# Sixteen moves of one-hot codes, issued from ScalarE's queue instead of SyncE's, in a clustered attention with a feed-forward layer

## The chip, the cores and the metric

The kernel runs on one core of a Trainium2 chip. The metric is the device time of one execution in microseconds; the kernel before takes 299.18 us (median of three runs, 299.0 to 299.66). Each engine has an instruction queue of its own and works through it in order; an instruction that waits holds up whatever stands behind it on its engine. PE is TensorE, DVE VectorE, ACT ScalarE, POOL GpSimd, SP SyncE. SP does no arithmetic: in this kernel it issues most of the transfers.

## The reference, cut to what matters

Attention over 4 batches, 8 heads, 768 positions of 64 numbers, in which a query sees a key only if both belong to the same of 16 clusters; then a SiLU layer over the heads put side by side.

```python
q_assign = np.argmax(np.einsum('bhsd,hcd->bhsc', q_n, c_n), axis=-1)
k_assign = np.argmax(np.einsum('bhsd,hcd->bhsc', k_n, c_n), axis=-1)
mask = q_assign[:, :, :, None] == k_assign[:, :, None, :]
scores = np.where(mask, scale * np.matmul(q, k.transpose(0, 1, 3, 2)), -1000000000.0)
attn = softmax(scores)                       # over the keys
x = (attn @ v).transpose(0, 2, 1, 3).reshape(B * S, H * D)
h = x @ w_in;  out = (h / (1 + exp(-h))) @ w_out
```

## The kernel before

**The work on one head.** A *job* is the rows of q and k of one head: jobs 0 to 7 are batch 0, 8 to 15 batch 1, and so on; two further jobs, `x0` and `x1`, hold half of the queries of batch 0 for four heads each. The rows are loaded (`raw`), split into a high and a low 16-bit half (`hi` L97, `lo` L110, tile `hl`) and transposed into the tile `ab`, which has 128 rows: on PE with an eviction in the opening (`tr`, `ev`), by a DMA transpose from SP in batch 1 (`xpose`, L121). From `ab` PE computes the sixteen logits of each row (L159); DVE takes the maximum (`mxn`, L183) and compares (`om`, L192), which gives a one-hot code for the cluster.

**The move.** The code has to stand below the data, in rows 64 to 79 of the same tile `ab`, because the score product (`qk_mm`, L325) then adds a large negative number wherever clusters differ. For that PE transposes the code into PSUM (`cd_mm`, L221, tiles `psN` or `psC`); `cd_ev` copies it into a tile `cd` of 80 or 96 partitions, on ACT (L232) or on DVE (L234); and a DMA (L235) carries `cd` into rows 64 to 79 of `ab`, 40 or 48 KB. This is done for sixteen jobs: 2 to 7, x0 and x1 in the opening, 8 to 15 in batch 1. No `qk_mm` that reads this `ab` can start before the move has landed. (Jobs 0 and 1 write their codes in place, and batches 2 and 3 take another way, with `c_move` on POOL.)

**What follows.** ACT turns each score tile into exponentials (`exp`, L330, tile `P`); the score tile `pS` has two buffers, so `qk_mm` of unit u waits for the exponential of unit u-2. PE multiplies with v (`pv`, L342); then come the first matrix of the layer (L390), tanh on ACT (L402), a gate on DVE (L405) and the second matrix (L417, L477).

**What sets the order.** It is written out by hand: `plan` is a list of words, each of which calls one helper, so every engine's order is that of the words. `ce2.A` is `cd_ev` of job 2 with the eviction on ACT, `ce5.D` that of job 5 on DVE; `xe0`, `xe1` are those of the x jobs. `ex4` is an exponential, `qk4` its product, `ht14` the DMA transpose of job 14, `r10` the loads of job 10, `vl6` a load of v. SP issues its DMAs in the order of the plan as well: a move stands on SP's queue behind all loads, transposes and stores that the plan names before it.

**The semaphores of the DMAs.** The program gives the transfers of SP and ACT eight semaphores in turn, DMAHW0 to DMAHW7 in the rows below. A transfer does not start before the one that had its semaphore last, eight transfers earlier in the plan, has landed. This wait is taken by the queue that issues the transfer.

Of the kernel before, what the change touches and what calls it, by code (L numbers as in the profile page):

```python
# [29 lines left out]
def kernel(  # L30
# [52 lines left out]
    raws, hls, abs_ = {}, {}, {}  # L83
# [141 lines left out]
    def cd_ev(job, eng):  # L225
        m = (job.n + 1) // 2
        cd = mp.tile([6 * HC, 256], f16, name="cd", bufs=4)
        psN = psNs.pop(job.name)
        o, i = cd[0 : m * HC], psN[0 : m * HC, 256:512]
        add = 0.0 if job.name[0] == "x" else kadd[0 : m * HC, m - 5 : m - 4]  # L230
        if eng == "A":
            nc.scalar.activation(out=o, in_=i, func=AF.Identity, bias=add, scale=OHV)  # L232
        else:
            nc.vector.tensor_scalar(out=o, in0=i, scalar1=OHV, scalar2=add, op0=ALU.mult, op1=ALU.add)  # L234
        nc.sync.dma_start(abs_[job.name][64 : 64 + HC, 0 : 2 * m, :].rearrange("p n c -> p (n c)"), o)  # L235
# [368 lines left out]
    def step(op, n, eng, banks):  # L604
# [225 lines left out]
```

## Time and profile before

| what | us |
|---|---|
| median of three runs | 299.18 |
| the three runs | 299.18, 299.66, 299.0 |
| span of the profiled execution, first to last instruction | 297.9 |
| PE busy | 288.7 |
| ACT busy | 233.2 |
| DVE busy | 223.8 |
| idle time of PE before score products (L325) | 2.2 |

The page gives no time for the profiled execution besides its span; the runs lie 1.1 to 1.8 us above it. Times in the profile count from the start of the span. The opening is the first 40 us or so, batch 1's codes are made between 60 and 95 us. "SPq" and "ACTq" are the queues that issue DMAs; the duration of such a row is the issue alone, and the landing is given apart.

### The profile page before, as it was taken

What the parts mean: (1) busy time and instruction counts of PE and PEld (TensorE: products, weight loads), DVE (VectorE), ACT (ScalarE), POOL (GpSimd) and SP (SyncE); (2) the same over time, 40 slices, a digit from 0 to 9 for tenths busy, and PEclk for the clock granted to TensorE, in tenths of its full rate; (3) what the DMA queues carried; (4) which work ended last, traced back from release to release, by engine and by line L of the source; (5) the groups of instructions that cost most, each with busy time, mean ns of one, the idle gap of its engine ahead of it and who ended that gap; (6) DMA issues with size and microseconds to landing.
All of it is one profiled execution on the core that took longest, in us unless ns stands there. A gap on an engine that the chain in (4) does not pass through costs nothing.

```text
span 297.9 us, 8577 instructions
## 1 busy us (share of the span) xinstructions
PE 288.7 (97%) x3433; PEld 212.6 (71%) x3433; DVE 223.8 (75%) x489; ACT 233.2 (78%) x406; POOL 68.7 (23%) x124
## 2 busy tenths in 40 slices
PE   7899999999979999999999999999999999999995
PEld 3767766666658887777866887767867886777684
DVE  5898849689979986989467897788656733666663
ACT  5998999965979878999789876898669768964731
POOL 2655804000227001334444024220420000000000
PEclk9999999999999999999999999999999999999999
DMA  6999999999997899795399535867221102211103
GB/s 214 286 256 247 179 201 176 193 247 216 171 300 178 171 176 257 176 151 131 102 202 213 164 66 114 256 165 113 51 89 35 26 2 74 82 29 35 39 19 125
DMA packets 75208, 44.13 MB, mean 148 GB/s; under 512 B 54288, under 2 KB 70960, under 8 KB 75168
## 3 DMA queue, kind: packets, MB, share of 16 engines
q1 hardware_dynamic: 70272, 35.75, 50.3%
q0 software_dynamic: 4608, 7.54, 13.5%
q8 instruction: 27, 0.44, 0.6%
q10 hardware_dynamic: 288, 0.30, 0.3%
q14 instruction: 13, 0.11, 0.1%
HBM read 27.30 MB, written 6.29 MB: 113 GB/s over the span
## 4 chain that ended last, share of the span: by engine, by line
PE 87%; DMA 5%; ACT 3%; DVE 3%; issue 1%; SPq 0%; ACTq 0%
PE ph L390 25%; PE pS L325 20%; PE xb L477 18%; PE pO L342 12%; PE psN L159 4%; PE yb L477 3%; PE po L417 2%; DMA ab<-cd 2%; DMA ab<-hl 1%; DMA raw<-in_q_dram 1%; DVE hl L112 1%; PE wb L477 1%; ACT P L330 1%; ACT hl L103 1%; PE pTq L135 1%
## 5 line engine op out<-in xcount | busy, mean ns | idle before, releaser
L330 ACT ACTIVATE P<-pS 128x768 f16<-128x768 f32 x192 | 151.0, 815 | 18.8 <-PE pS L325 17.4
L390 PE MATMUL ph<-xt,win_s 128*128 128x384 f16 x512 | 96.1, 326 | 0.0
L405 DVE SCALAR_TENSOR_TENSOR gt<-tn,ph 128x384 f16<-128x384 f32 x128 | 68.2, 549 | 31.9 <-ACT tn L402 31.0
L325 PE MATMUL pS<-ab 128*128 128x384 f16 x384 | 86.7, 326 | 2.2 <-DMA ab<-cd 1.6
L402 ACT ACTIVATE tn<-ph 128x384 f32<-128x384 f32 x128 | 61.6, 499 | 13.9 <-PE ph L390 10.5
L390 PEld LDWEIGHTS <-win_s 128*128 128x128 f16 x512 | 49.4, 98 | 31.0 <-issue 0.3
L325 PEld LDWEIGHTS <-ab 128*128 128x128 f16 x384 | 34.2, 98 | 18.3 <-DMA ab<-cd 2.2
L342 PEld LDWEIGHTS <-P 128*128 128x128 f16 x1152 | 39.8, 97 | 3.8 <-DVE cd L234 0.4
L342 PE MATMUL pO<-vt,P 128*128 128x65 f16 x1152 | 41.2, 193 | 0.0
L477 PEld LDWEIGHTS <-gt 128*128 128x128 f16 x352 | 34.1, 98 | 6.5
L112 DVE SCALAR_TENSOR_TENSOR hl<-raw,hl 128x768 f16<-128x768 f32 (+3 forms) x35 | 32.0, 916 | 0.8 <-ACT hl L103 0.5
L105 POOL TENSOR_SCALAR hl<-raw 128x768 f16<-128x768 f32 (+1 forms) x9 | 19.5, 2167 | 47.2 <-DVE gt L405 30.7
L477 PEld LDWEIGHTS <-s 128*128 128x128 f16 x264 | 25.5, 98 | 4.7
L199 POOL TENSOR_SCALAR od<-od 128x96 f16<-128x96 f16 x16 | 8.4, 526 | 63.3 <-DVE od L192 63.2
L499 ACT ACTIVATE ot<-xb 128x256 f32<-128x256 f32 x33 | 12.7, 385 | 12.9 <-PE xb L477 12.6
L477 PE MATMUL xb<-wout_s,gt 128*128 128x256 f16 x176 | 22.6, 273 | 0.0
L159 PEld LDWEIGHTS <-ab 128*128 128x128 f16 x544 | 18.9, 97 | 4.1 <-DMA ab<-hl 0.5
L477 PE MATMUL xb<-wc,s 128*128 128x256 f16 x160 | 20.7, 272 | 0.0
L159 PE MATMUL psN<-stk,ab 128*128 128x16 f16 (+1 forms) x544 | 20.1, 184 | 0.1
L354 DVE TENSOR_TENSOR xn<-pO,zr 128x384 f16<-128x384 f32 x32 | 17.8, 557 | 1.1
L490 DVE TENSOR_TENSOR s<-gt 128x1024 f16<-128x1024 f16 x22 | 15.5, 712 | 1.3 <-PE xb L477 1.0
L212 POOL DMA_DIRECT2D ab<-cdt x16 | 9.0, 564 | 19.8 <-PE pS L325 5.2
(93 smaller groups left out, 258.2 us busy)
## 6 DMA issues: line engine op xcount, KB each, us to landing
raw<-in_k_dram SPq DMA_DIRECT2D x31, 192.0 KB, 3.9
raw<-in_q_dram SPq DMA_DIRECT2D x24, 192.0 KB, 3.5
out_dram<-ot SPq DMA_DIRECT2D x18, 256.0 KB, 2.9
vn<-in_v_dram SPq DMA_DIRECT2D x19, 192.0 KB, 4.7
vn<-in_v_dram POOLq DMA_DIRECT2D x13, 192.0 KB, 3.4
win_s<-in_moe_w_in_dram POOLq DMA_DIRECT2D x8, 256.0 KB, 6.8
wout_s<-in_moe_w_out_dram POOLq DMA_DIRECT2D x4, 512.0 KB, 9.2
out_dram<-ot SPq DMA_DIRECT2D x12, 128.0 KB, 1.8
```

What stands on the lines that cost most here:

```text
L105: nc.gpsimd.tensor_scalar(out=o, in0=i, scalar1=QS, scalar2=None, op0=ALU.mult)
L112: nc.vector.scalar_tensor_tensor(out=hl[:, s, 1, :], in0=raws[job.name][:, s, :], scalar=QS, in1=hl[:, s, 0, :], op0=ALU.mult, op1=ALU.sub ...
L159: nc.tensor.matmul(L[:, n % 2, :, n // 2], ab[:, i, :], stk[:, job.groups[i // 3][0], x : x + w], start=(x == 0), stop=(x + w == 2 * HC),)
L325: nc.tensor.matmul(pS[:, e, 0:HALF], abs_[kj.name][:, kn, :], rhs, start=True, stop=True)
L330: nc.scalar.activation(out=P, in_=pst.pop(u)[:, :, 0:HALF], func=AF.Exp, bias=0.0, scale=ESC)
L342: nc.tensor.matmul(o[:, (2 * t + h) * VW : (2 * t + h + 1) * VW], Ps[i + h, c, j // 2][:, j % 2, ts(t, 128)], vtb[(i + h) % 13][:, j, 0:VW ...
L354: nc.vector.tensor_tensor(out=xn, in0=ov[:, :, 0:D], in1=zr.unsqueeze(2).to_broadcast([128, 2 * NM, D]), op=ALU.mult)
L390: nc.tensor.matmul(ph[:, 0:HALF], win_s[:, r, ts(fb, 128)], xts[b, c][:, r, :], start=(r == 0), stop=(r == NR - 1))
L402: nc.scalar.activation(out=tn, in_=phs[b, c, fb][:, 0:HALF], func=AF.Tanh, bias=0.0, scale=0.5)
L405: nc.vector.scalar_tensor_tensor(out=gt[:, fb, NM * c : NM * c + NM, :].rearrange("p t n -> p (t n)"), in0=tns.pop((b, c, fb)), scalar=1.0 ...
L477: nc.tensor.matmul(o, self.lhs(l, f), self.rhs(r, f), start=(f == 0 and opens), stop=(f == HB - 1), skip_group_check=True)
L490: nc.vector.tensor_tensor(out=o, in0=a, in1=b_, op=op)
```

## The change

All sixteen moves are issued by ACT's queue. The letters in the plan say where the eviction and the issue run: `.A` was eviction on ACT and move from SP, now `.B` is eviction on ACT and move from ACT; `.D` was eviction on DVE and move from SP, now `.C` is eviction on DVE and move from ACT. The evictions keep their engines: ten are on ACT (ce2, ce3, ce4, ce7, xe1, ce8, ce10, ce9, ce14, ce15), six on DVE (ce5, ce6, xe0, ce11, ce12, ce13). No word of the plan changes its place.

```diff
-        if eng == "A":
+        if eng in "AB":
             nc.scalar.activation(out=o, in_=i, func=AF.Identity, bias=add, scale=OHV)
         else:
             nc.vector.tensor_scalar(out=o, in0=i, scalar1=OHV, scalar2=add, op0=ALU.mult, op1=ALU.add)
-        nc.sync.dma_start(abs_[job.name][64 : 64 + HC, 0 : 2 * m, :].rearrange("p n c -> p (n c)"), o)
+        (nc.scalar if eng in "BC" else nc.sync).dma_start(abs_[job.name][64 : 64 + HC, 0 : 2 * m, :].rearrange("p n c -> p (n c)"), o)
...
-        evk7.A ex7 qk8 cm5 ex8 xl0 ge6 cm6 ce5.D xq0.0 ce6.D evq7.D xp0.1 xu0.D qk9 xw0.D v1 vl12 ex9 v4 v7 pa0.3 qk10
+        evk7.A ex7 qk8 cm5 ex8 xl0 ge6 cm6 ce5.C xq0.0 ce6.C evq7.D xp0.1 xu0.D qk9 xw0.D v1 vl12 ex9 v4 v7 pa0.3 qk10
```

**ACT, the opening, jobs 3 and 4** (`cd_508` and `cd_513` are their codes, `P_532` is ex4); in brackets stand the semaphores that a row waits for.

```order
 L330 ACTIVATE P_494<-pS_445 128x768 [waits PE_49]
 L232 ACTIVATE cd_508<-psN_392,kadd_88 80x256 [waits DVE_49,PE_49]
+L235 DMA ab_332<-cd_508 16x5x256 [waits DMAHW7_49,Activation_49]
 L232 ACTIVATE cd_513<-psN_452,kadd_88 80x256 [waits DVE_49,PE_49]
+L235 DMA ab_426<-cd_513 16x5x256 [waits DMAHW3_49,Activation_49]
 L330 ACTIVATE P_532<-pS_490 128x768
 L330 ACTIVATE P_610<-pS_516 128x768 [waits PE_49]
```

Each move stands right behind its own eviction and waits for it (Activation_49); the next eviction and the exponentials stand behind the moves.

**ACT, the opening, jobs 5, 6, 7 and x0** (`cd_636`, `cd_647` and `cd_786` are evicted by DVE; `P_630` is ex8, `P_666` ex9, `P_789` ex12).

```order
 L330 ACTIVATE P_630<-pS_625 128x768 [waits PE_49]
+L235 DMA ab_476<-cd_636 16x5x256 [waits DMAHW0_49,DVE_49]
+L235 DMA ab_519<-cd_647 16x5x256 [waits DMAHW1_49,DVE_49]
 L330 ACTIVATE P_666<-pS_659 128x768 [waits PE_49]
 L330 ACTIVATE P_714<-pS_683 128x768 [waits PE_49]
 L330 ACTIVATE P_716<-pS_711 128x768 [waits PE_49]
-L232 ACTIVATE cd_768<-psN_688,kadd_88 80x256 [waits DVE_49,DMAHW6_49,PE_49,Activation_49]
+L232 ACTIVATE cd_768<-psN_688,kadd_88 80x256 [waits DMAHW7_49,DVE_49,PE_49]
+L235 DMA ab_598<-cd_768 16x5x256 [waits DMAHW2_49,Activation_49]
+L235 DMA ab_639<-cd_786 16x6x256 [waits DMAHW3_49,DVE_49]
 L330 ACTIVATE P_789<-pS_760 128x768 [waits PE_49]
```

Two moves of DVE's codes now stand between ex8 and ex9, and two moves ahead of ex12. Each waits for a semaphore of a transfer of SP.

**SP, the opening, as it stands now** (`raw_499` is job 10, `raw_589` job 9, `vn` loads of v).

```order
L94 DMA raw_424<-in_q_dram 128x4x192 [waits DMAHW2_49,DVE_49]
L92 DMA raw_499<-in_q_dram 128x384 [waits DMAHW3_49]
L92 DMA raw_499<-in_k_dram 128x384 [waits DMAHW4_49]
L264 DMA vn_502<-in_v_dram 128x384 [waits DMAHW5_49,Pool_49]
L264 DMA vn_562<-in_v_dram 128x384 [waits DMAHW6_49,Pool_49]
L264 DMA vn_585<-in_v_dram 128x384 [waits DMAHW1_49,DMAHW0_49,Activation_49]
L92 DMA raw_589<-in_q_dram 128x384 [waits DMAHW1_49]
```

The moves are gone from between these loads. Which transfer a move on ACT waits for can be read here: ce4's (DMAHW3) for `raw_499<-in_q`, ce5's (DMAHW0) for `vn_585`, ce6's (DMAHW1) for `raw_589<-in_q`.

**ACT, batch 1, job 11** (`cd_1781` is evicted by DVE, `P_1784` is ex49).

```order
 L402 ACTIVATE tn_1767<-ph_1762 128x384 [waits DVE_49,PE_49]
+L235 DMA ab_1386<-cd_1781 16x6x256 [waits DMAHW7_49,DMAHW4_49,DVE_49]
 L330 ACTIVATE P_1784<-pS_1773 128x768 [waits PE_49]
 L330 ACTIVATE P_1786<-pS_1776 128x768 [waits PE_49]
-L402 ACTIVATE tn_1813<-ph_1805 128x384 [waits DVE_49,PE_49]
```

**SP at the same place of the plan, as it stands now** (`hl_1620` is job 14, `hl_1685` job 15).

```order
L121 DMA_TRANSPOSE ab_1594<-hl_1589 128x12x128 [waits DMAHW0_49,DVE_49,PE_49]
L92 DMA raw_1627<-in_q_dram 128x384 [waits DMAHW2_49,DMAHW1_49]
L92 DMA raw_1627<-in_k_dram 128x384 [waits DMAHW3_49]
L121 DMA_TRANSPOSE ab_1675<-hl_1620 128x12x128 [waits DMAHW4_49,DVE_49]
L121 DMA_TRANSPOSE ab_1688<-hl_1685 128x12x128 [waits DMAHW5_49,DVE_49,PE_49]
```

The move of job 11 left SP's queue for a place ahead of ex49 on ACT's; there it waits for DMAHW4, which job 14's transpose (`ab_1675`) had last. The orders of PE, DVE and POOL are the same as before.

More of the change, by code (lines that the diff above doesn't have):

```diff
@@ L724 @@
         j2.1 mx0 ge0 evq1.A hi3.A lo3 evk1.A ct0.32 ctk0 tr2.10 ctq0 hi5.A evk2.A L1.3 lo4 xr0 evq2.A tr3.21 evq3.A
-        qk0 ex0 mx1 L2.0 ge1 ct1.13 ctq1 evk3.D qk1 ex1 L3.2 mx2 ge2 cm2 ce2.A ctk1 lo5 xr1 tr4.13 evk4.D evq4.A mx3
-        qk2 qk3 hi7.P v0 ge3 L4.0 mx4 ge4 tr5.31 ex2 qk4 v3.A ex3 hi6.P lo6 r10 vl7 cm3 evq5.D evk5.D ce3.A cm4 ce4.A
+        qk0 ex0 mx1 L2.0 ge1 ct1.13 ctq1 evk3.D qk1 ex1 L3.2 mx2 ge2 cm2 ce2.B ctk1 lo5 xr1 tr4.13 evk4.D evq4.A mx3
+        qk2 qk3 hi7.P v0 ge3 L4.0 mx4 ge4 tr5.31 ex2 qk4 v3.A ex3 hi6.P lo6 r10 vl7 cm3 evq5.D evk5.D ce3.B cm4 ce4.B
         qk5 tr6.23 evk6.D ex4 L5.1 v5 evq6.D j1.2 qk6 vl2 L6.2 vl6 mx5 r9 r11 w1 lo7 tr7.03 ex5 ge5 qk7 xh0.A ex6 mx6
-        evk7.A ex7 qk8 cm5 ex8 xl0 ge6 cm6 ce5.D xq0.0 ce6.D evq7.D xp0.1 xu0.D qk9 xw0.D v1 vl12 ex9 v4 v7 pa0.3 qk10
-        w3 L7.1 w7 qk11 ex10 ex11 xL0.0 xM0 mx7 ge7 cm7 pb0 qk12 xm0 xg0 xh1.D ce7.A v2 xc0 pc0 xe0.D ex12 qk13 pa1.0
+        evk7.A ex7 qk8 cm5 ex8 xl0 ge6 cm6 ce5.C xq0.0 ce6.C evq7.D xp0.1 xu0.D qk9 xw0.D v1 vl12 ex9 v4 v7 pa0.3 qk10
+        w3 L7.1 w7 qk11 ex10 ex11 xL0.0 xM0 mx7 ge7 cm7 pb0 qk12 xm0 xg0 xh1.D ce7.B v2 xc0 pc0 xe0.C ex12 qk13 pa1.0
         qk14 pc1 nm0 pt0.3 w2 ex13 qk15 xl1 w5 v6.D pb1 hi8.D nm1 ex14 qk16 ex15 qk17 ex16 ex17 hi10.P w10 xq1.1 xp1.2
         xu1.D qk18 qk19 pa2.0 pb2 w6 w4 od0 v12.D xw1.D ex18 qk20 pt1.2 hi9.D pe1.D pc2 nm2 ex19 qk21 xL1.2 ex20 w8
-        xM1 ex21 qk22 qk23 pt2.0 ex22 ex23 xm1 px3.1 qk24 pe0.D lo8 xg1 xc1 py3 qk25 ex24 qk26 pe2.D a1.0 xe1.A nm3
+        xM1 ex21 qk22 qk23 pt2.0 ex22 ex23 xm1 px3.1 qk24 pe0.D lo8 xg1 xc1 py3 qk25 ex24 qk26 pe2.D a1.0 xe1.B nm3
         pt3.1 pe3.D a0.2 ex25 ex26 qk27 ex27 e1 e4.1 e0 t4 g4 vl10 qk28 t0 g0 qk29 ex28 e6.3 t6 g6 ex29 vl11.P e3.1 t3
@@ L737 @@
         g15 qk41 ex41 t7 g2 r15 wc6 e9.0 qk42 t9 b0.3 qk43 g7 b1 ex42 wc0 qk44 g12 g9 hi13.D L8.1 ex43 b2 qk45 lo13
-        mx8 L10.2 ge8 cm8 mx10 ex44 b3 ex45 ce8.A wc1 ge10 bo0 pv6.1 nm6 qk46 l9.0 ht13 cm10 vl15 ls9 mx9 wc2 ge9 qk47
-        hi12.A lo12 vl13 ht12 wc12 b4.3 ce10.A ex46 pt6.2 b5 cm9.0 ex47 hi14.A ce9.A pe6.A lo14 r16 pv7.1 nm7 b6 ht14
+        mx8 L10.2 ge8 cm8 mx10 ex44 b3 ex45 ce8.B wc1 ge10 bo0 pv6.1 nm6 qk46 l9.0 ht13 cm10 vl15 ls9 mx9 wc2 ge9 qk47
+        hi12.A lo12 vl13 ht12 wc12 b4.3 ce10.B ex46 pt6.2 b5 cm9.0 ex47 hi14.A ce9.B pe6.A lo14 r16 pv7.1 nm7 b6 ht14
         pt5.0 pe5.D qk48 hi15.D lo15 ht15 v10.D pt7.1 pe7.A r17 ex48 b7 bo1 e24.0 e18.1 t24 g24 t18 L11.2 wc8 mx11 g18
-        ge11 e22.3 t22 hi16.P e21.0 t21 g22 v11.D v8.D g21 qk49 qk50 cm11 ce11.D ex49 ex50 l12.3 vl9 ls12 e29.1 r18
+        ge11 e22.3 t22 hi16.P e21.0 t21 g22 v11.D v8.D g21 qk49 qk50 cm11 ce11.C ex49 ex50 l12.3 vl9 ls12 e29.1 r18
         t29 g29 e20.0 t20 g20 e27.2 v13.A mx12 t27 g27 e23.3 ge12 qk51 t23 ex51 l13.1 ls13 qk52 ex52 g23 mx13 e19.0
-        t19 e25.2 g19 t25 cm12.1 qk53 ex53 e26.3 g25 v15.D qk54 t26 ex54 ce12.D vl16.P g26 e16.0 t16 e30.2 qk55 ge13
+        t19 e25.2 g19 t25 cm12.1 qk53 ex53 e26.3 g25 v15.D qk54 t26 ex54 ce12.C vl16.P g26 e16.0 t16 e30.2 qk55 ge13
         g16 vl17.P l15.3 ls15 t30 ex55 lo16 r20 qk56 e28.0 t28 ex56 vl14 g30 e17.3 g28 L14.1 qk57 qk58 t17 g17 ex57
-        cm13.2 mx14 e31.0 ce13.D ex58 qk59 t31 v9.D mx15 S3 m1.3 ge14 od2 hi17.A ex59 g31 ge15 wc13 pv8.2 cm14 lo17
-        r19 ce14.A ht17 qk60 nm8 ex60 S1 qk61 ex61 m7 qk62 ex62 cm15.0 ce15.A wc7 S13 pv9.1 z0 qk63 ex63 S2 nm9 wc14
+        cm13.2 mx14 e31.0 ce13.C ex58 qk59 t31 v9.D mx15 S3 m1.3 ge14 od2 hi17.A ex59 g31 ge15 wc13 pv8.2 cm14 lo17
+        r19 ce14.B ht17 qk60 nm8 ex60 S1 qk61 ex61 m7 qk62 ex62 cm15.0 ce15.B wc7 S13 pv9.1 z0 qk63 ex63 S2 nm9 wc14
         v16.D wc9 wc15 wc10 qk64 m11.2 ex64 qk65 m2.0 qk66 ex65 m17 ex66 hi18.P qk67 qk68 lo18 z10 ex67 ht16 vl21.P
```

## The prediction

> **What bounds the kernel now.** I began with the page's busy times and its chain of work that ended last.
>
> ```profile
> span 297.9 us, 8577 instructions
> PE 288.7 (97%) x3433; PEld 212.6 (71%) x3433; DVE 223.8 (75%) x489; ACT 233.2 (78%) x406; POOL 68.7 (23%) x124
> ...
> PE 87%; DMA 5%; ACT 3%; DVE 3%; issue 1%; SPq 0%; ACTq 0%
> ```
>
> PE is the bound: busy for 288.7 of 297.9 us and 87% of the chain. So all idle time of PE is worth 9.2 us, while whatever newly stops PE is added in full. Next, the view of the tile `cd`: what the sixteen moves cost now.
>
> ```profile
> L235 SPq DMA_DIRECT2D ab<-cd x16: 561/567/992, 15.4 to 94.5; - x16
> L234 DVE TENSOR_SCALAR cd<-psC,kadd x2: 465/472/479, 82.1 to 88.4; 96x256 f16<-96x256 f32 x2
> ...
> DMA to landing us min/median/max: 2.7/4.5/7.3
> ```
>
> An issue takes 0.57 us of SP, and one move lands 4.5 us after it. Which move PE has to wait for is told by the chain of waits (its first two rows) and the timelines of DVE and of SP's queue:
>
> ```profile
> 82.05 5.36 DMA ab<-cd
> 87.46 0.82 PE L325 MATMUL pS<-ab 128*128 128x384 f16 x4 [1.57 <-DMA ab<-cd]
> 75.41 0.47 DVE L234 TENSOR_SCALAR cd<-psN,kadd 96x256 f16<-96x256 f32 x1
> 75.25 5.13 SPq L121 DMA_TRANSPOSE ab<-hl  x2
> ```
>
> It is the move of job 11: DVE had its code ready at 75.88 (75.41 + 0.47), but SP was in two transposes and some loads and issued it at 82.05; it landed at 87.41. **1.57 us is what the change can gain.** Now what it loads ACT with: the windows of the opening and of the stretch of job 8 to 10's moves.
>
> ```profile
> 14.80:40.40 25.60, 24.31 (x419) 18.03 (x416) 21.78 (x50) 23.32 (x36) 14.85 (x27) 1.00 1.00 219
> 60.00:72.00 12.00, 12.00 (x172) 7.92 (x168) 10.76 (x24) 7.31 (x13) 0.00 (x0) 1.00 1.07 235
> ```
>
> The columns after the length are PE, weight loads, DVE, ACT. In the opening ACT is busy 23.32 of 25.60 us: 2.28 us idle, while PE waits for its exponentials in turn. From 60 to 72 it has 4.69 us idle.
>
> **The change part by part.** *A move behind its own eviction on ACT* (ten). ACT's timeline shows the spacing now (its last row is ex9 to ex11):
>
> ```profile
> 14.87 0.46 ACT L232 ACTIVATE cd<-psN,kadd 80x256 f16<-80x256 f32 x1
> 15.29 0.49 ACT L144 ACTIVATE ab<-pTq 128x384 f16<-128x384 f16 x1
> ...
> 17.54 0.83 ACT L232 ACTIVATE cd<-psN,kadd 80x256 f16<-80x256 f32 x2
> ...
> 23.97 2.33 ACT L330 ACTIVATE P<-pS 128x768 f16<-128x768 f32 x3
> ```
>
> The next activation starts 0.42 us after an eviction. With the move between, it waits for the end (0.46), the issue (0.57) and two hand-overs of some 0.03: 1.10, so **0.68 us each**.
>
> *A move of a code that DVE evicted* (six). ACT's queue runs ahead of its arithmetic, as a wait shows ahead of a cast of the opening:
>
> ```profile
> L103 ACTq EVENT_SEMAPHORE  x1: 17/17/17, 19.0 to 19.0; - x1
> L103 ACT ACTIVATE hl<-raw x1: 848/848/848, 19.7 to 19.7; 128x768 f16<-128x768 f32 x1
> ```
>
> The wait was passed at 19.0, under the exponential before. So an issue of 0.57 fits under an exponential (0.81 alone in the row of 26.92 below, 2.33 for three at 23.97: 0.76 apart) and costs nothing **if code and semaphore are there**; if not, everything behind it stands. When the semaphores come free is read from the timeline of SP's queue and from the view of single transfers (KB, and us from issue to landing, at the end; job 10's load, a load of v, job 9's, and job 14's transpose).
>
> ```profile
> 16.73 0.51 SPq L92 DMA_DIRECT2D raw<-in_q_dram  x1
> 20.68 0.42 SPq L92 DMA_DIRECT2D raw<-in_q_dram  x1
> raw<-in_q_dram SPq DMA_DIRECT2D x1, 192.0 KB, 4.2
> vn<-in_v_dram SPq DMA_DIRECT2D x1, 192.0 KB, 6.4
> raw<-in_q_dram SPq DMA_DIRECT2D x1, 192.0 KB, 7.0
> ab<-hl SPq DMA_TRANSPOSE x1, 5.7
> ```
>
> *Opening.* Five evicted on ACT: 5 x 0.68 = 3.4. ce4's move waits for job 10's load, 16.73 + 4.2 = 20.9 now; without ce2's move SP issues it some 0.7 us (that move's issue and gap) sooner, so 20.2. ACT gets there at 17.54 + 0.83 + 2 x 0.68 = 19.7: **0.5** (0 to 1.2). ce5's and ce6's moves wait for a load of v and for job 9's, now 26.6 (issued at 20.2) and 20.68 + 7.0 = 27.7; sooner by what SP no longer does, near 25.6 and 26.5. With 0.57 for the issue ex9 starts at 27.1. It started at 23.97, and the three moves ahead of it (3 x 0.68 = 2.0) would alone put it at 26.0: **1.1** (0.3 if both have landed, 2.4 if both land as now). x0's move waits for DVE, which evicts until 27.81 (27.40 + 0.41); ex12 behind it then starts at 28.45 instead of 26.92 (timelines of ACT, DVE, PE):
>
> ```profile
> 26.92 0.81 ACT L330 ACTIVATE P<-pS 128x768 f16<-128x768 f32 x1 [0.17 <-PE pS L325]
> 27.40 0.41 DVE L234 TENSOR_SCALAR cd<-psN 96x256 f16<-96x256 f32 x1
> 28.24 0.49 PE L325 MATMUL pS<-ab 128*128 128x384 f16 x2
> ```
>
> **1.5** (0.6 to 1.5, since PE is fed from two buffers). Together 3.4 + 0.5 + 1.1 + 1.5 = 6.5. What covers a part: the 2.28 us idle, and a lead of exponentials over their products, which I estimate at 0.5 us from the last fence (the exponential of 26.92 ends at 27.73, a product of scores starts at 28.24). 6.5 - 2.28 - 0.5 = **+3.7** (1.5 to 6.2); the cover is then used up.
>
> *Jobs 8, 10, 9.* 3 x 0.68 = 2.0 lie in 4.69 us of idle time: **0** (to 0.5).
>
> *Job 11.* Behind its move stand ex49, ex50 and the tanh that feed PE (timelines of ACT and PE; last, the page's groups of the tanh and the gate, 499 and 549 ns each):
>
> ```profile
> 74.39 1.51 ACT L330 ACTIVATE P<-pS 128x768 f16<-128x768 f32 x2
> 77.79 0.49 PE L325 MATMUL pS<-ab 128*128 128x384 f16 x2
> 78.11 0.51 PE L159 MATMUL psN<-stk,ab 128*128 128x32 f16 x12
> L402 ACT ACTIVATE tn<-ph 128x384 f32<-128x384 f32 x128 | 61.6, 499 | 13.9 <-PE ph L390 10.5
> L405 DVE SCALAR_TENSOR_TENSOR gt<-tn,ph 128x384 f16<-128x384 f32 x128 | 68.2, 549 | 31.9 <-ACT tn L402 31.0
> ```
>
> The move waits for DVE (75.88) and for job 14's transpose. That is issued at 75.25 and lands 5.7 later, at 80.97. SP loses three moves before it, 0.57 and a gap each, some 2.0 us: issue at 73.25, landing some 4.9 later (the transposes around take 4.1 to 6.0) near 78.2. The move is then done at 78.8 and ex49 starts at 78.85, 4.5 us late. It ends at 79.66, so PE's product of 77.79 stands 1.9 us; the logits of 78.11 need a gate whose tanh comes after ex50: 78.85 + 1.51 + 0.50 for the tanh + 0.55 for the gate = 81.4. **+3.3** (1.0 if DVE's eviction is the last, 6.0 if the transpose lands as now).
>
> *The gain.* Job 11's move then leaves by 78.8 and lands near 83 at 4.5, in a program that is 3.3 us later itself, so that its product comes at 86 or after: the 1.57 us go, **-1.6** (-1.2 if the landing is slow).
>
> *Jobs 12 to 15.* ACT's timeline has the places of ce12's move, ahead of the first row's tanh, and of ce13's, between the two exponentials of the second:
>
> ```profile
> 82.49 1.00 ACT L402 ACTIVATE tn<-ph 128x384 f32<-128x384 f32 x2
> ...
> 88.00 1.51 ACT L330 ACTIVATE P<-pS 128x768 f16<-128x768 f32 x2 [1.74 <-PE pS L325]
> ```
>
> ce12's move waits for DVE until 82.6 (82.1 + 0.47) and takes 0.57: the tanh comes at 83.2 instead of 82.49, of which I take **+0.5** (0 to 0.7), the rest under the lead. ce13's holds the second exponential from 88.70 to 89.5 (88.4 + 0.48, then 0.57): 0.8. ce14 and ce15 cost 0.68 each: 2.2. Less some 0.6 of cover (the 0.5 us of lead again, and gaps), **+1.6** (0.7 to 2.3).
>
> **The sum**: 3.7 + 0 + 3.3 - 1.6 + 0.5 + 1.6 = **+7.5 us**. The profiled span is 297.9; the median of the runs is 299.2, 1.3 us above it, and I keep that distance: 297.9 + 7.5 + 1.3 = **306.7 us**.
>
> **The rivals.** *Faster (0.07).* SP's queue is all that delays job 11's code: had its semaphore come free before 76.5 and the issues of the opening run under the activations, only the gain stays, 299.2 - 1.6 = 297.6. For it: SP holds that code for 6.2 us. Against: an issue behind its own eviction has nothing to run under, and ACT has 2.28 us to give in the opening. It decides at the five evictions there: below 0.45 us each they vanish in that idle time. *Nothing moves (0.04)*: the opening costs 1.5, job 11's wait is as short as DVE allows with the semaphores of SP free, and the gain takes it back, about 299.2. *Only the issues cost (0.11)*: the semaphores have come free wherever ACT arrives, as SP runs ahead: 1.5 + 1.0 - 1.6 + 0.5 + 0.7, some +2, so 301. *Issues of two queues exclude each other (0.06)*: if a move on ACT had to wait until SP's issue is done, three of them beside transposes (2.6 us each, 5.13 for two, less the 0.5 paid above) would add 6.3: 313. The rows of the start speak against it, where both queues issue at once and neither takes longer:
>
> ```profile
> 0.72 0.41 ACTq L92 DMA_DIRECT2D raw<-in_k_dram  x1
> 0.73 0.39 SPq L544 DMA_DIRECT2D craw<-in_centroids_dram  x1
> ```
>
> The Trainium skill (Perfetto Trace Analysis, "DMA Instruction — HWDGE (DVE, Sync)") does describe a descriptor generator shared by two queues and locked for one issue at a time; by that rule this rival would hold, and these two rows don't agree, though they are plain loads and no transposes.
>
> **How the numbers follow.** Forecast +7.5 with 0.72. The parts are independent, and all low (+2) or all high (+14) at once is unlikely. The range of 301.5 to 312.5 leaves out the faster rival, no change and half of the issue-only case, and most of the exclusion: about 2 in 10. A measurement tells 0.2%, 0.6 us, from no change: faster 0.07, same 0.04, slower 0.89.
>
> **What would show it.** Right: ACT's queue with a gap of over 3 us before ex49 that job 14's transpose ends; PE waiting for exponentials in the opening; 0.7 us more behind each eviction with a move; the 1.57 us before job 11's product gone. Wrong: no gap before ex49 (the transpose landed earlier), or moves on ACT that take far from 0.57 us, or PE's idle time in the opening not longer by 3 us or so.

## The result and the profile after

The changed kernel takes **309.49 us** (median of four executions, 307.29 to 313.51) against 299.35 us. The ratio is 1.0319, 95% interval 1.0262 to 1.0376: some 9.5 us slower (7.8 to 11.3). Ratios, here and below, leave out every execution that lies over 1.5% above the fastest of its kernel, while medians and ranges keep it: 313.51 us of these four, and below 307.57 (batch 1 alone), 424.16 at a clock of 0.658 (job 11 alone), 312.73 (the changed kernel again), 312.77 (job 4 back on SP) and 303.66 (job 11's move ahead of job 15's transpose). The prediction was 306.7 us, range 301.5 to 312.5.

First the page of the profiled execution: span, busy time of the engines, and the granted clock of TensorE in 40 slices, in tenths of full speed.

```profile
span 308.6 us, 8562 instructions
PE 293.3 (95%) x3433; PEld 215.0 (70%) x3433; DVE 221.7 (72%) x489; ACT 233.6 (76%) x406; POOL 68.0 (22%) x124
...
PEclk9996999999979999999999999999999999999999
```

The span is 10.7 us longer, and it comes in two parts. PE is idle for 15.3 us (308.6 - 293.3) where it was 9.2: 6.1 us more. And PE is *busy* for 4.6 us more with the same 3433 matmuls. A change that only makes engines wait cannot do that; the 6 and the 7 in the last line, at a clock that stood at full speed in the kernel before, say what it is. The rows of the tile `cd` answer to those of before:

```profile
L235 ACTq DMA_DIRECT2D ab<-cd x16: 568/569/692, 15.2 to 104.8; - x16
...
DMA to landing us min/median/max: 2.1/4.2/6.1
```

An issue costs ACT what it cost SP (569 ns against 567), and a move lands as fast as before. So neither the issue nor the transfer got worse. What did is told by PE's timeline, at four of its products and logits (start, duration in us, what; in brackets the idle time before):

```profile
23.51 0.80 PE L325 MATMUL pS<-ab 128*128 128x384 f16 x2 [3.30 <-DMA raw<-in_q_dram]
...
85.19 0.49 PE L325 MATMUL pS<-ab 128*128 128x384 f16 x2 [1.00 <-ACT P L330]
86.87 0.64 PE L159 MATMUL psN<-stk,ab 128*128 128x32 f16 x12 [1.19 <-DMA ab<-cd]
...
96.18 0.81 PE L325 MATMUL pS<-ab 128*128 128x384 f16 x4
```

Two new stops, one in the opening and one in two pieces ahead of job 11; the last row is job 11's product, and its wait of 1.57 us is gone. In the first row two products take 0.80 us, which took 0.49 before. (The trace names a move as the releaser of the third row. DVE's gate of the tanh before it started at 86.26, and where the changed kernel was profiled again, the same stop of 1.19 us is put down to the gate: it is the gate that these logits wait for, as the prediction had it.) ACT's timeline at the two places shows who stood where:

```profile
19.57 0.47 ACT L232 ACTIVATE cd<-psN,kadd 80x256 f16<-80x256 f32 x1 [0.94 <-PE pTq L135]
22.04 0.57 ACTq L235 DMA_DIRECT2D ab<-cd  x1
22.65 0.81 ACT L330 ACTIVATE P<-pS 128x768 f16<-128x768 f32 x1 [2.60 <-DMA raw<-in_q_dram]
...
83.71 0.57 ACTq L235 DMA_DIRECT2D ab<-cd  x1
84.33 0.81 ACT L330 ACTIVATE P<-pS 128x768 f16<-128x768 f32 x1 [3.32 <-PE ph L390]
```

Job 4's code was ready at 20.04 (19.57 + 0.47), and its move left at 22.04, after a load of job 10 had landed. Job 11's move left at 83.71, after job 14's transpose. (The trace names the matrix product that came before as the releaser of the last row; but the issue stands between, and SP's queue and the view of single transfers say what it waited for.)

```profile
15.59 0.61 SPq L92 DMA_DIRECT2D raw<-in_q_dram  x1
raw<-in_q_dram SPq DMA_DIRECT2D x1, 192.0 KB, 6.4
78.54 4.02 SPq L121 DMA_TRANSPOSE ab<-hl  x2
ab<-hl SPq DMA_TRANSPOSE x1, 5.1
```

15.59 + 6.4 = 22.0, and 78.54 + 5.1 = 83.6: each time the move follows the landing at once. Last, the windows at the two stops: PE, weight loads, DVE, ACT, POOL, then the granted clock, the DMA share and GB/s.

```profile
22.00:24.00 2.00, 0.49 (x2) 0.26 (x2) 0.00 (x0) 1.35 (x2) 0.48 (x2) 0.56 0.73 212
24.00:26.00 2.00, 2.00 (x32) 1.72 (x31) 1.12 (x3) 2.00 (x4) 2.00 (x4) 0.50 0.81 244
26.00:28.00 2.00, 2.00 (x15) 1.53 (x14) 0.97 (x4) 1.85 (x3) 0.43 (x1) 0.50 0.97 210
28.00:30.00 2.00, 2.00 (x31) 1.61 (x29) 1.50 (x4) 0.65 (x1) 0.00 (x0) 0.73 0.59 191
...
86.00:88.00 2.00, 1.13 (x15) 0.80 (x15) 1.74 (x4) 2.00 (x6) 0.00 (x0) 0.77 1.00 319
88.00:90.00 2.00, 2.00 (x8) 0.99 (x7) 1.76 (x6) 1.68 (x3) 0.00 (x0) 0.50 0.75 271
90.00:92.00 2.00, 2.00 (x14) 1.20 (x13) 1.31 (x4) 1.29 (x3) 1.08 (x1) 0.87 0.01 4
```

**With each stop the granted clock falls to 0.50**: from 22.24 us, while PE still stands, to 29.06, and from 87.09 to 90.50 (the edges by the trace's record of the clock). PE is busy for 9.0 of these 10.2 us; half of that, 4.5 us, is the longer busy time. It was no term of the prediction.

Since the order on PE is the same in both kernels, the lag of any of its instructions can be read off the two traces. Its growth from place to place says what each step cost (times in us):

| PE instruction | start before | start after | lag | what lies between |
|---|---|---|---|---|
| transpose ahead of the stop | 18.90 | 19.06 | +0.2 | job 2's issue, covered |
| product of the first stop | 19.78 | 23.51 | +3.7 | the stop |
| product | 23.45 | 28.59 | +5.1 | clock 0.5 |
| product behind job 7 and x0 | 29.62 | 35.56 | +5.9 | issues and waits of jobs 5, 6, 7, x0 |
| L390, ahead of job 11's stops | 75.19 | 81.43 | +6.2 | x1, jobs 8 to 10 |
| logits (L159) | 78.11 | 86.87 | +8.8 | the two stops |
| transpose of a code (L221) | 80.09 | 90.50 | +10.4 | clock 0.5 |
| job 11's product | 87.46 | 96.18 | +8.7 | the gain |
| product behind job 15 | 95.89 | 106.58 | +10.7 | jobs 12 to 15 |

### The profile page after: what moved, and what is told of

The parts are those of the page before. It is cut to its first block, busy times and chain, and to the rows that moved or that the text cites. A ratio compares the mean times of both kernels' runs of the same rounds, so it can differ in the third digit from the quotient of the medians.

```text
span 308.6 us, 8562 instructions
## 1 busy us (share of the span) xinstructions
PE 293.3 (95%) x3433; PEld 215.0 (70%) x3433; DVE 221.7 (72%) x489; ACT 233.6 (76%) x406; POOL 68.0 (22%) x124
## 4 chain that ended last, share of the span: by engine, by line
PE 80%; DMA 7%; ACT 5%; DVE 3%; issue 2%; ACTq 1%; SPq 0%; DVEq 0%
PE ph L390 24%; PE pS L325 18%; PE xb L477 17%; PE pO L342 10%; PE psN L159 3%; PE yb L477 3%; DMA ab<-cd 3%; ACT P L330 2%; DMA raw<-in_q_dram 2%; DMA ab<-hl 2%; DVE hl L112 1%; PE wb L477 1%; PE po L417 1%; ACT hl L103 1%; DMA raw<-in_k_dram 1%
## 5 line engine op out<-in xcount | busy, mean ns | idle before, releaser
L390 PE MATMUL ph<-xt,win_s 128*128 128x384 f16 x512 | 97.4, 329 | 0.0
L325 PE MATMUL pS<-ab 128*128 128x384 f16 x384 | 88.4, 330 | 7.3 <-ACT P L330 4.0
L402 ACT ACTIVATE tn<-ph 128x384 f32<-128x384 f32 x128 | 61.6, 502 | 14.6 <-PE ph L390 11.3
L390 PEld LDWEIGHTS <-win_s 128*128 128x128 f16 x512 | 49.8, 99 | 31.9 <-issue 1.6
L325 PEld LDWEIGHTS <-ab 128*128 128x128 f16 x384 | 34.7, 99 | 24.3 <-issue 8.6
L105 POOL TENSOR_SCALAR hl<-raw 128x768 f16<-128x768 f32 (+1 forms) x9 | 18.8, 2092 | 41.9 <-DMA raw<-in_k_dram 35.7
L159 PEld LDWEIGHTS <-ab 128*128 128x128 f16 x544 | 19.3, 97 | 5.6 <-issue 1.8
L159 PE MATMUL psN<-stk,ab 128*128 128x16 f16 (+1 forms) x544 | 20.4, 185 | 1.5 <-DMA ab<-cd 1.2
L168 DVE TENSOR_REDUCE L<-psN 128x192 f32<-128x384 f32 x20 | 11.1, 553 | 3.6 <-PE psN L159 3.4
```

The costliest lines, as they stand in the source:

```text
L105: nc.gpsimd.tensor_scalar(out=o, in0=i, scalar1=QS, scalar2=None, op0=ALU.mult)
L159: nc.tensor.matmul(L[:, n % 2, :, n // 2], ab[:, i, :], stk[:, job.groups[i // 3][0], x : x + w], start=(x == 0), stop=(x + w == 2 * HC),)
L325: nc.tensor.matmul(pS[:, e, 0:HALF], abs_[kj.name][:, kn, :], rhs, start=True, stop=True)
L390: nc.tensor.matmul(ph[:, 0:HALF], win_s[:, r, ts(fb, 128)], xts[b, c][:, r, :], start=(r == 0), stop=(r == NR - 1))
L402: nc.scalar.activation(out=tn, in_=phs[b, c, fb][:, 0:HALF], func=AF.Tanh, bias=0.0, scale=0.5)
```

## The experiments

The theory after this: ACT's queue takes over the waits that SP's queue used to take, PE stops, and a stop costs twice, since the clock falls with it. The rival: it is simply the time of sixteen issues on a busy engine.

**The two halves alone.** Only the opening, or only batch 1, has the new letters:

```diff
-ce2.A ce3.A ce4.A ce5.D ce6.D ce7.A xe0.D xe1.A
+ce2.B ce3.B ce4.B ce5.C ce6.C ce7.B xe0.C xe1.B
```

> The eight moves of the opening (jobs 2 to 7, x0, x1) from ScalarE's queue, the eight of batch 1 from SyncE's as before. Theory (waits and clock: ScalarE's queue stands at landings of other transfers, TensorE stops over 3 us and its granted clock halves for some us afterwards): the lag that the changed kernel has over the kernel before at 60 us of its trace, +6 us, stays, and job 11's wait of about 1.6 us stays too: 305 us, with a stop of TensorE near 20 to 23.5 us and a clock of 0.5 behind it. Rival (only the issues on ScalarE cost, 0.6 to 0.7 each): 8 x 0.65 less 2.8 us of cover, +2.4: 301.7 us, no stop over 1 us.

```diff
-ce8.A ce10.A ce9.A ce11.D ce12.D ce13.D ce14.A ce15.A
+ce8.B ce10.B ce9.B ce11.C ce12.C ce13.C ce14.B ce15.B
```

> The eight moves of batch 1 (jobs 8 to 15) from ScalarE's queue, the opening as before. Theory (waits and clock): job 11's move waits on ScalarE until job 14's transpose has landed, TensorE stands over 2 us and its clock halves; +4 us there with the clock, -1.6 for the wait that goes, +2 for jobs 12 to 15: +4.5, 303.8 us. Rival (only the issues cost): 0.3 for job 11, -1.6, +1.5 for jobs 12 to 15: 299.5 us.

Measured beside 298.64 us: the opening 302.66 (ratio 1.0141, 1.0095 to 1.0186), batch 1 303.33 (1.0148, 1.01 to 1.0196). By the ratios the halves cost 4.2 and 4.4 us, together 8.6 of the 9.5. The opening came out between the two theories: the stop is there, and the clock did not fall. Batch 1 came out near the theory's 303.8, but the profiled execution has both stops ahead of the logits (1.13 and 1.19 us) at a clock of 1.00, so its time came about without the clock's part.

PE's timeline and the window behind it, opening alone:

```profile
22.32 0.48 PE L325 MATMUL pS<-ab 128*128 128x384 f16 x2 [2.19 <-DMA raw<-in_q_dram]
22.00:24.00 2.00, 1.68 (x33) 1.39 (x33) 0.59 (x2) 2.00 (x4) 1.67 (x5) 1.00 0.93 288
```

A stop of 2.2 us, the same load as its releaser, and a clock of 1.00. So the stop was there in both traces of this opening so far, and whether the clock falls depends on its length or its moment; the traces settle which further down. Here three executions of four kept a mean clock of 1.000, in batch 1 three of four.

**The issues' time alone.** All moves stay on SP. Where a move would stand on ACT's queue, ACT runs an activation that nothing reads:

```diff
+nz = {"Y": 656, "Z": 600}.get(eng)
+nz and nc.scalar.activation(out=zz[:, 0:nz], in_=zz[:, 0:nz], func=AF.Copy, bias=0.0, scale=1.0)
```

> All moves from SyncE as before; in each place where a move stands on ScalarE's queue after the change, ScalarE runs an activation of 656 (behind its own eviction) or 600 columns (code evicted by VectorE) instead, which nothing reads: 0.55 to 0.6 us of ScalarE each, without any wait. Rival (the issues' time on ScalarE is the cost): 16 x 0.57 = 9 us less about 4 us of cover, +5 and more, and 1.6 of it isn't given back: 304 to 306 us. Theory (waits and clock): the occupancy is the smaller part, +2 to +3.5 us: 301.2 to 302.7 us, with the clock at 1.00 throughout.

Measured: 302.76 us (1.0149, 1.0098 to 1.02), +4.1; at the upper edge of the theory's figure, below the rival's, though the interval (+2.9 to +6.0, up to 304.6 us) reaches into the rival's range. The view of the tile `zz` gives the length of the stand-ins, against an issue's 569 ns:

```profile
L236 ACT ACTIVATE zz<-zz x16: 694/740/767, 15.3 to 98.8; 128x656 f16<-128x656 f16 x10, 128x600 f16<-128x600 f16 x6
```

The stand-ins are no exact copy. From an eviction to the next activation pass 1.00 us with a stand-in between (18.12 to 19.12) and 1.11 with a move (104.33 to 105.44 in the changed kernel), so behind an eviction they are a little short; between two exponentials a stand-in takes 0.7 us (two from 24.98 to 26.38), while an issue that has nothing to wait for runs under one. So the mere time of the issues is worth some 4 us, as an estimate. That is a large share, and not the whole: the change costs 9.5 although it also wins job 11's 1.6 us back.

**Job 11's move alone.**

```diff
-ce11.D
+ce11.C
```

> Only job 11's move from ScalarE's queue. Theory (waits and clock): SyncE gets to job 14's transpose hardly sooner than before, so it lands near 80.5 and ScalarE stands from 75.9 to 81; the product of 77.8 and the logits of 78.1 come 4 to 6 us late, the clock halves behind that (+1.5), the 1.6 us before job 11's product go: +4 to +6, 304 us, more than the whole of batch 1 gave to job 11. Rival (only the issue costs): 0.3 - 1.6 = -1.3, 298 us.

This missed. Measured: 299.9 us (1.0041, 1.0021 to 1.0061), +1.3 where +4 to +6 was expected. ACT's timeline:

```profile
75.57 0.67 ACTq L235 DMA_DIRECT2D ab<-cd  x1
76.29 1.51 ACT L330 ACTIVATE P<-pS 128x768 f16<-128x768 f32 x2 [2.38 <-PE ph L390]
```

The move left at 75.57, only 0.27 us after DVE had its code ready (75.30), and long before job 14's transpose landed (80.78). The eight semaphores go round in the order in which the program is laid out, and that order shifts when other moves change their queue: here job 11's move has the semaphore of job 9's move, which landed at 75.50. My expectation had carried the semaphore of the full change over to another program. It makes a useful pair, though: with job 14's semaphore the exponentials behind the move stood 3.3 us, with job 9's 2.4 us, and even then PE lost 1.2 us ahead of the logits and gained 1.55 at job 11's product. That would make nothing or a small gain; where the measured +1.3 comes from isn't shown (the profiled executions of this kernel and of the kernel before have spans of 297.7 and 297.9 us, but stem from different comparisons).

**The changed kernel again**, beside three variants of it on the same chip.

> The changed kernel itself, for its spread and beside the three others of this comparison. Expected: TensorE's stop of 2 to 3.3 us near 20 us (job 4's move waits on ScalarE for job 10's load) and the wait of ScalarE for job 14's transpose in every run; a granted clock below 1 in most runs, and the longer runs are those with the lower clock; 307 to 311 us.

Measured: 309.7 us (306.87 to 312.73, six executions; ratio 1.034, 1.0289 to 1.039). The spread follows the clock: 306.87 us at a mean of 0.999, 307.84 at 0.994, 308.26 at 0.993, 311.15 at 0.989, 311.43 at 0.983 (and 312.73 at 0.984). Both waits were in the profiled execution again (stops of 1.98 us and of 1.48 and 1.19), with one dip of the clock instead of two.

**The first stop filled.** Ten matmuls that nothing reads. The product that stops is `qk6`; they stand one product ahead of it, so that `qk5` and the work behind it move into the stop:

```diff
-qk5
+j10.1 qk5
```

> The changed kernel with ten matmuls that nothing reads on TensorE ahead of the product that stops in the opening, about 0.22 us each, so that the stop of 3.3 us is cut to some 1.1. Theory (a stop brings the granted clock down): the clock stays at 1.00 from 22 to 30 us, and the time falls by the 1.7 to 1.8 us that the dip cost there: below the changed kernel by 1 to 2 us, with fewer or no clocks under 0.99. Rival (the clock dips by itself, or for what the whole chip does): the dip is there as before, and the time is the same or up to 1 us longer.

Measured: 307.39 us (306.06 to 310.43), by the ratios (1.0299 and 1.034) 1.2 less than the changed kernel beside it; their intervals, 1.0256 to 1.0343 and 1.0289 to 1.039, overlap. The longest stop of PE left at that place is 0.62 us. The clock is clearer: exactly 1.000 in four of six executions and 0.994 in two, against 0.983 to 0.999 without the fillers. The windows behind the place:

```profile
22.00:24.00 2.00, 1.68 (x38) 1.26 (x35) 2.00 (x6) 2.00 (x4) 1.54 (x3) 1.00 0.84 244
24.00:26.00 2.00, 1.58 (x21) 1.19 (x19) 1.99 (x5) 2.00 (x4) 1.68 (x3) 1.00 0.85 176
```

More work on PE, and no more time; that it is less isn't clear of the spread.

**Job 4's move back on SP.**

```diff
-ce4.B
+ce4.A
```

> The changed kernel, but job 4's move is issued by SyncE again; the semaphores move on, so that job 3's move now waits for a load that is long there. Theory (waits): the stop at 20 us goes (below 1 us), the first dip of the clock with it; the lag in the opening falls from 6 to about 3: 3 us less than the changed kernel, 306 us. Rival (the issues' time on ScalarE is the cost): 0.7 us less, 309 us.

Measured: 308.21 us (1.0311, 1.027 to 1.0352), by the ratios 0.9 less than the changed kernel where 3 was expected, and not clear of the spread. The first stop went (0.54 us are left), but another came. ACT and PE:

```profile
23.98 3.42 ACTq L235 DMA_DIRECT2D ab<-cd  x2
27.45 0.81 ACT L330 ACTIVATE P<-pS 128x768 f16<-128x768 f32 x1 [2.72 <-DVE om L192]
28.31 0.48 PE L325 MATMUL pS<-ab 128*128 128x384 f16 x2 [2.22 <-ACT P L330]
```

With the semaphores moved on by one, job 6's move got that of a load of v, issued at 21.59, which landed at 26.76; the move left at 26.84. The wait was not removed, it went to the next move in the queue.

**Job 11's move on POOL**, whose transfers have semaphores of their own:

```diff
-ce11.C
+ce11.G hi16.P
```

`G` is eviction on DVE and issue from POOL; `hi16.P` stood ahead of it.

> The changed kernel, but job 11's move is issued by GpSimd, whose transfers have semaphores of their own (a cast of job 16 goes behind it on that queue). Theory (waits): ScalarE no longer stands for job 14's transpose, TensorE's stops of 1.0 and 1.2 us before the product and the logits go and with them the dip behind, while the gain on job 11's own product stays: 3 to 4 us less than the changed kernel, 305.5 to 306.5 us. Rival (the issues' time): 0.3 us less, 309 us.

Measured: 305.94 us (1.0223, 1.0194 to 1.0252), by the ratios 3.5 less than the changed kernel, as expected. Both stops ahead of the logits are gone, and the gain at job 11's product stays.

**A stop without any move.** All moves on SP; nine activations that nothing reads on ACT behind job 4's eviction.

```diff
+[nc.scalar.activation(out=zz, in_=zz, func=AF.Copy, bias=0.0, scale=1.0) for _ in range(9 if eng == "Y" else 0)]
...
-ce4.A
+ce4.Y
```

> The kernel before, all moves on SyncE, with nine activations of 512 columns that nothing reads on ScalarE behind job 4's eviction, some 0.5 us each: TensorE stops for about 4 us in the opening, without any change in the transfers. Theory (a long stop brings the granted clock down): 0.5 for some 6 us behind the stop, in every run or nearly; +4.2 for the stop and +1.8 for the clock, less what the program takes back later: +5.5, 304 us, clocks of 0.99 and less. Rival (the clock dips by itself in the changed kernel): +4, 302.7 us, clock 1.00.

Measured: 304.46 us (1.0184, 1.0157 to 1.0211), +5.3. PE stopped for 4.5 us, and the mean clock was 0.987 to 0.993 in all six executions, where the 23 of the kernel before had 0.998 to 1.000. The windows:

```profile
24.00:26.00 2.00, 1.76 (x23) 0.95 (x24) 0.00 (x0) 2.00 (x4) 1.14 (x3) 0.50 0.73 240
26.00:28.00 2.00, 2.00 (x20) 1.49 (x17) 1.42 (x3) 1.85 (x4) 1.76 (x3) 0.50 0.74 107
28.00:30.00 2.00, 2.00 (x19) 1.87 (x18) 1.14 (x3) 1.33 (x2) 0.00 (x0) 0.50 0.14 25
30.00:32.00 2.00, 2.00 (x46) 1.57 (x44) 1.31 (x3) 1.47 (x2) 0.26 (x2) 0.98 0.25 56
```

The clock falls without any move issued from ACT: the stop is enough.

**The same stop, filled**, with twenty matmuls:

```diff
-qk5
+j20.1 qk5
```

> The same stop, but TensorE runs twenty matmuls that nothing reads (0.22 us each, 4.4 us) ahead of the product that waits for ScalarE. Theory: the clock stays at 1.00, +4 to +4.4: 302.8 us, 1 to 2 us less than with the bare stop, though TensorE does more. Rival: no difference between the two beyond 0.5 us.

This one was badly built. Measured: 310.7 us (1.039), clocks of 0.983 to 0.989. The fillers read the tile `zz`, which the nine activations write, so they waited for them, PE stopped 6.6 us instead of 4.5, and the fillers then ran at half clock. It says nothing on whether filling helps.

**Two ways to the gain without ACT.** Job 11's move alone on POOL, or ahead of job 15's transpose on SP, all others as before:

```diff
-hi16.P ... ce11.D
+ce11.G hi16.P
```

> The kernel before, with job 11's move alone issued by GpSimd ahead of the cast of job 16, all other moves on SyncE. Theory (ScalarE's share of the change is all cost, the gain is job 11's wait alone): the move leaves near 76.5 and lands by 82, TensorE's wait of 1.6 us goes and nothing takes its place: -1.2 to -1.6, 297.2 us. Rival (another transfer of that stretch is late next, or GpSimd's issue is slow): no change, 298.7 us.

```diff
-ht15 ... ce11.D
+ce11.D ht15
```

> The kernel before, all moves on SyncE, with job 15's transpose put behind job 11's move on SyncE's queue. Theory: the move leaves some 2.5 us sooner, near 79.5, and lands by 85: -1.2 to -1.6, 297.2 us. Rival: job 15's transpose, now 1 us later, or the transfers around it are late next: no change, 298.7 us.

Measured: 298.19 us (0.9984, 0.9964 to 1.0004) and 299.89 us (1.0013, 0.999 to 1.0035), beside 299.17. POOL issued at once, and PE's wait is gone from the trace (from that of the second kernel too):

```profile
75.58 0.59 POOL L205 DMA_DIRECT2D ab<-cd  x1 [26.95 <-DVE cd L234]
85.05 0.81 PE L325 MATMUL pS<-ab 128*128 128x384 f16 x4
```

Yet the medians differ by 1.0 us at most, and neither is clear of no change. The executions of the kernel before spread from 297.61 to 300.73 us, and only one of them was profiled; how long job 11's move holds PE in the others isn't known. Whether the whole 1.57 us can be had stays open.

## Why the prediction was right, and what it missed

The direction, the places and the waits were right, and the time lay in the range; a term was missing, and others made up for each other. By its own steps, with the growth of the lag from the table:

| step | predicted | in the trace |
|---|---|---|
| opening | +3.7 | +5.9, of which 1.4 behind the stop at clock 0.5 |
| x1, jobs 8, 10, 9 | 0 | +0.3 |
| job 11's wait on ACT | +3.3 | +4.2, of which 1.65 at clock 0.5 |
| the gain at job 11's product | -1.6 | -1.7 |
| jobs 12 to 15 | +2.1 | +2.0 |
| sum | +7.5 | +10.7; without the two stretches at half clock +7.6 |

**The missing term is the clock.** The step that failed is the one that took a stop of PE for its own length: "whatever newly stops PE is added in full". It is added, and the clock stands at 0.50 for 6.8 and 3.4 us with it, which made 3.1 us of lag here (1.4 + 1.65). That is the share of the profiled execution, at a mean clock of 0.983; 308.34 and 307.29 us had 0.992 and 0.994, and the two halves alone cost 8.6 us together with a clock of 1.000 in six of their eight executions, 1.1 more than the +7.5. The one execution of the changed kernel that kept a clock of 0.999 took 306.87 us, 8.1 above the 298.74 beside it. Why this wasn't seen: the kernel before has a clock of 1.00 in every window that was read, with a stop of 1.57 us among them.

The Trainium skill (TensorE: Matmul & The Clock Gate, "What's actually happening") states that the clock goes to half after an idle window of some 3.4 us and that the window runs freely, without regard to the kernel. The half agrees with the 0.50 of these windows, a stop of 4.5 us brought it on in all six executions, and the six dips of the kept traces lasted 3.41 us (three), the length of that window, or 6.83 (three), twice it. As a bound for the idle time the 3.4 us don't agree: stops of 1.98 us, and of 1.00 and 1.19 us close together, brought a dip as well, while stops of 2.19 (the opening alone) and 2.22 us (job 4 back on SP) did not.

The moment decides, by these traces. Within each of them the recorded changes of the clock lie whole multiples of 3.41 us apart; in the changed kernel 58.03 us, 17 of them, pass between the two dips. Cut into steps on that grid, PE's busy time (the first number behind the length) is, in the step just before a dip of the changed kernel and of the changed kernel again, then in the two steps that share the stop of the opening alone, and last at the stop of job 4 back on SP:

```profile
18.82:22.24 3.42, 1.39 (x31) 1.08 (x29) 2.14 (x6) 0.47 (x1) 0.00 (x0) 1.00 1.00 317
18.63:22.04 3.41, 1.69 (x32) 1.29 (x31) 2.44 (x7) 1.18 (x3) 0.00 (x0) 1.00 1.05 340
...
17.70:21.11 3.41, 2.06 (x36) 1.47 (x34) 3.18 (x8) 1.32 (x3) 0.00 (x0) 1.00 1.06 335
21.11:24.52 3.41, 1.89 (x34) 1.46 (x34) 1.11 (x2) 3.07 (x5) 2.19 (x5) 1.00 0.98 290
24.34:27.75 3.41, 1.75 (x41) 1.41 (x39) 1.95 (x6) 0.69 (x2) 0.00 (x0) 1.00 1.00 299
```

The six steps ahead of a dip have 0 to 1.69 us of PE's work. Every other step at full clock in the fourteen traces, from the clock's first record at 3.9 to 7.2 us on, has 1.74 or more; only in the last 10 us of the program did one with 1.48 stay at full clock. So what brought the clock down here is not a stop's length, but that PE stood for about half of one step; a stop of 2.2 us does that or not, as it falls on the grid. The clock came back after a step with at least 3.15 us of work; with 1.90 to 2.43 us it stayed down for a second step.

**Inside the opening terms were mis-sized and made up for each other.** Job 4's wait was put at 0.5 us (0 to 1.2) and was 2.0 (20.04 to 22.04). Up to that stop the terms are 3 x 0.68 + 0.5 = 2.5 us before the cover, and the lag grew by 3.7. Behind it they are 1.1 for jobs 5 and 6, 0.68 for job 7 and 1.5 for x0, 3.3 us before the cover, and the lag grew by only 0.8 (5.1 to 5.9), besides the clock. So it is in part luck that +7.6, the sum without the clock, comes so near to +7.5. The step behind job 4's figure, that SP's earlier issue brings an earlier landing, was wrong: the load was issued 1.1 us sooner (15.59 against 16.73) and landed 1.1 us later (22.0 against 20.9); the sixteen DMA engines were full, with a share of 1.01 to 1.05 in each window from 16 to 22 us. In the four other traces with this wait (the opening alone, the changed kernel again, the first stop filled, job 11's move on POOL) the move left at 20.8 to 21.0, so the load landed about as late as before, and the wait was 0.9 to 1.1 us, inside the stated 0 to 1.2. What made it a further 1.1 us late in the first profile isn't known. The Trainium skill (DMA: Bandwidth & Descriptors, "Issuing engines are not separate DMA queues") says that all queues run on the same sixteen engines and that issuing from several saves the time of issuing alone; these landings agree. Jobs 5 and 6, by contrast, were held by DVE's eviction and not by the loads.

**Job 11** went as described: ACT idle for 3.32 us, ended by job 14's transpose, and 2.5 us of lag without the clock against +3.3. The semaphore isn't all of that idle time: ACT was through at 81.01, DVE had the code ready at 82.34 (81.86 + 0.48) and the transpose had landed at 83.6, so some 1.3 us each went to DVE and to the transpose, and the rest to the issue. The kernel with that one move on POOL shows it: 3.5 us less.

**The rivals.** *Only the issues cost* was given 0.11 and +2 us. The stand-ins on ACT cost 4.1 without the gain, so about +2.5 with it, near its figure; the rest of the 9.5 is put down to waits and clock by subtraction. *Faster* had SP's queue as the only delay of job 11's code. The wait did go, but even when nothing else was moved and no semaphore was late (job 11 alone), the time was 1.3 us longer. *Issues that exclude each other*: the longest of the sixteen issues on ACT took 0.69 us, and those beside transposes of SP no more than the rest (0.58 beside the transpose of 74.75), so there was no such lock here. The section of the Trainium skill that the prediction cites there names the queues of VectorE and SyncE, not ScalarE's.

## What to carry to other kernels

Before an issue is moved to another queue, list what it will wait for there, the semaphore that it inherits included, and who stands behind it; then expect the wait to move on to the next issue when one is taken out. On SP, which does no arithmetic, the wait of job 11's code cost PE 1.57 us; on ACT the waits of the issues stopped PE for 3.3 and 2.2 us. And price a stop of TensorE above its length: look at the granted clock of the windows behind it, and in more than one execution, since the same stop brings the clock down in some and not in others. Where a stop can't be avoided, matmuls that nothing reads and that depend on nothing may be cheaper than silence; the one trial that worked kept the clock up, and its gain of 1.2 us isn't clear of the spread.

## What was not expected of the hardware

With a stop of TensorE of 2 to 4.5 us the granted clock went to 0.50 for 3.41 or 6.83 us, though PE was busy again for most of that, and two products took 0.80 us instead of 0.49. It is not the same in every execution: five of the changed kernel had mean clocks from 0.983 to 0.999 and times from 311.43 to 306.87 us, so one and the same program moves, along with its clock, by near half of what the change cost. And a load that is issued 1 us sooner into full DMA engines did not land sooner.
